# Attention with two gated MLPs: low parts of weights on VectorE, the PSUM banks of a pair apart, a re-timed engine order

## The chip, the cores and the metric

The kernel runs on one core of a Trainium2 chip. The metric is the device time of one execution in microseconds, as the median of several runs. A core has TensorE (PE in the profile, with PEld for its weight loads), VectorE (DVE), ScalarE (ACT), GpSimd (POOL) and SyncE (SP, which here issues nearly all DMAs). TensorE writes to PSUM, in banks of 512 fp32 columns on each partition, and the other engines read the results from there.

## What is computed

```python
def attention(q, k, v, cap):                 # 4 batches, 12 heads, 448 positions, 64 per head
    s = cap * tanh(q @ k.T / sqrt(64) / cap)
    e = exp(s - max(s));  return (e / (sum(e) + 1e-9)) @ v
x = attention(...)                           # 1792 tokens x 768
h = relu(x @ w_in);  x = (h * h) @ w_out     # 768 -> 2048 -> 768
g = sigmoid(x @ w_gate)                      # 768 -> 1536
out = (g * (x @ w_val)) @ w_out2             # 1536 -> 768
```

## The kernel before

**Precision.** A product of fp32 matrices is made of three fast matmuls: both operands are split into a high part (`hi`, rounded by a copy on ScalarE) and a low part (`lo = x - hi`), and lo·hi, hi·lo and hi·hi are added up in PSUM (L785, L787, L788). For a weight block, `place_w` has ScalarE write the high part `wh`, and `low` (L774) then has GpSimd write `wl`, the low part, by one subtraction over 128x384 or 128x768 elements. For activations VectorE makes the low part (`gx`, `gy`, `b`, `t`, by the helper at L240).

**Stages.** Attention runs over 24 pairs of heads. For a pair, TensorE makes the scores (`scores`, in three rotating PSUM tiles `so`, `si`, `se`), ScalarE takes tanh and exp (`pt`), TensorE multiplies by v (`pv`, L405, four steps), and then sums the rows of `pt` by matmuls with ones (`totals`, L420). The products and the sums of a pair lie in the two banks of one PSUM tile `pv`. VectorE copies the products out into `xe[:, 0]` once the four steps are done and the sums into `xe[:, 1]` after `totals` (both by L249); only after the second copy is the tile given back (`flow.put("pvb")`), and the next pair's first v step needs it. The normalisation then goes by small DMAs (`sg`, `rd`, `th`).

The two MLPs follow in four stages (two halves of the tokens for each MLP). Blocks are multiplied with seven products instead of eight (a Strassen scheme), so sums and differences of weights (`sums`, on VectorE) and of activations (`t`, `g`) are made first. The weights come as 64-bit words: they are loaded (`w`), turned into fp32 by five steps on VectorE (L627 to L635; in the MLP stages the first of them is on ScalarE), written to DRAM, and read back as `pair` when needed.

**What sets the order.** The order in which each engine's instructions stand is fixed when the program is built. The class `Flow` holds a small event model: a job yields an engine, a length and a rank, and waits for events or buffers; each engine takes the waiting job with the lowest rank and, among equals, the oldest. The lengths come from formulas (`act`, `dve`, `dvep`, `dve1`, `landing`), and the instruction is written to the engine at the moment that the model starts it. TensorE's own order is a list: in attention, the items S (a score tile), V (a v step) and Q (the sums) of `order`; behind it the MLP's `units`, in turn. `pick` starts an attention item when the model has its inputs, and otherwise the next unit when that one is ready. On the chip each engine then runs its list in that order and waits at the head of it. The formulas of before lengthen VectorE's work while GpSimd is busy (`shared`).

**Sigmoid.** ScalarE's first sigmoid is at the start of the third stage, the gate of the second MLP; its function table is loaded there.

Of the kernel before, what the change touches and what calls it, by code (L numbers as in the profile page):

```python
# [32 lines left out]
LATE = 1.0, 2.0, 0  # L33
# [27 lines left out]
class Flow:  # L61
# [4 lines left out]
    LAG = 0.06  # L66

    def __init__(self, have):
# [3 lines left out]
        self.queue = {e: [] for e in ("ACT", "DVE", "POOL", "SP")}  # L72
        self.free = {e: True for e in self.queue}
        self.end = dict.fromkeys(self.queue, 0.0)
# [37 lines left out]
    def serve(self, engine):  # L112
# [5 lines left out]
        length = length() if callable(length) else length  # L118

        def end():  # L120
            self.free[engine] = True
            self.at(self.now + self.LAG, lambda: self.step(job))
            self.serve(engine)

        self.end[engine] = self.now + length
        self.at(self.now + length, end)
# [23 lines left out]
    @staticmethod  # L150
    def act(n):
        return 0.23 + n * 0.00083

    def dve(self, n):
        return lambda: self.shared(0.15 + n * 0.00104, 2.0)

    def dve1(self, n):
        return lambda: self.shared(0.16 + n * 0.0005, 1.5)
# [7 lines left out]
    def dvep(n):  # L166
        return 0.15 + n * 0.00105


    def landing(self, size, store=False, rate=330e3):  # L170
        begin = max(self.now + (1.5 if store and size > 2e5 else 0.7 if store else 1.3), self.pipe)
        self.pipe = begin + size / rate
        return self.pipe + 0.9 - self.now
# [3 lines left out]
def attn_mlp_kernel(ctx: ExitStack, tc: tile.TileContext, qk, v, cap, w1, w2, wg, wv, wo, out):  # L177
# [33 lines left out]

    ones = T("att", "ones", [P, SR])
# [3 lines left out]
    for x in range(WARM):  # L216
        nc.tensor.matmul(out=bank2("pv", "pv")[:SR, 0, :S], lhsT=ones, rhs=warm, start=True, stop=True)
    head = T("att", "head", [P, 2, SR])
    for j in range(2):
# [4 lines left out]
        "sb": 3, "pvb": 1, "v": NV, "qkh": 2, "qk": 2, "pt0": PT, "pt1": PT, "xe": XE, "th": TH, "sg": 2,  # L224
# [20 lines left out]
    def post(out, bank, sb, op=ALU.add, rank=0):  # L245
        return on("DVE", flow.dvep(cols(out)), lambda: nc.vector.tensor_tensor(out=out, in0=sb, in1=bank, op=op), rank)  # L246

    def copy_ps(out, in_, rank=0):
        return on("DVE", flow.dvep(cols(out)), lambda: nc.vector.tensor_copy(out, in_), rank)  # L249
# [5 lines left out]
    def dma(out, in_, size, store=False, rate=330e3, issue=0.42, rank=1):  # L255
# [1037 lines left out]
```

## Time and profile before

| | us |
|---|---|
| median of 3 runs (1147.27 to 1152.98) | 1149.09 |
| the profiled execution: its time | 1153.2 |
| its span, from the first to the last instruction | 1151.4 |
| TensorE busy | 1105.2 |
| VectorE busy | 886.5 |
| ScalarE busy | 685.1 |
| GpSimd busy | 502.8 |

The span is 1.8 us shorter than the execution's own time. Attention ends at about 208 us of the span. A row of a timeline tells when an instruction (or a run of equal ones) started, how long it took, its engine, its line and tiles and, in brackets, how long the engine sat idle before it and what ended that. Instructions of one engine overlap a little: the next VectorE instruction starts some 0.08 us before the one before it is reported ended. Matmuls of 448 columns start 0.20 us apart at the full clock, though each is reported as 0.36 us long.

### The profile page before, as it was taken

What the parts mean: (1) busy time and instruction counts of PE and PEld (TensorE: products, weight loads), DVE (VectorE), ACT (ScalarE), POOL (GpSimd) and SP (SyncE); (2) the same over time, 40 slices, a digit from 0 to 9 for tenths busy, and PEclk for the clock granted to TensorE, in tenths of its full rate; (3) what the DMA queues carried; (4) which work ended last, traced back from release to release, by engine and by line L of the source; (5) the groups of instructions that cost most, each with busy time, mean ns of one, the idle gap of its engine ahead of it and who ended that gap; (6) DMA issues with size and microseconds to landing.
All of it is one profiled execution on the core that took longest, in us unless ns stands there. A gap on an engine that the chain in (4) does not pass through costs nothing.

```text
span 1151.4 us, 16365 instructions
## 1 busy us (share of the span) xinstructions
PE 1105.2 (96%) x5706; PEld 919.1 (80%) x5706; DVE 886.5 (77%) x1178; ACT 685.1 (60%) x1153; POOL 502.8 (44%) x364
## 2 busy tenths in 40 slices
PE   9999999998999999999999989799899899999997
PEld 4444444788988999999999879699798799999996
DVE  4586787987989479679889999769998646257467
ACT  6877898665554557675747556455445355555351
POOL 0000100444444435354636266567564656565543
PEclk9999999999999999999999999899999999999999
DMA  4677785597777275888896344374456843241322
GB/s 140 207 247 259 244 264 172 189 306 231 238 243 247 104 249 195 293 300 282 313 318 206 133 169 160 111 249 162 156 184 245 296 147 98 83 125 48 123 70 96
DMA packets 83986, 227.44 MB, mean 198 GB/s; under 512 B 11840, under 2 KB 29888, under 8 KB 83904
## 3 DMA queue, kind: packets, MB, share of 16 engines
q1 hardware_dynamic: 83904, 226.40, 58.3%
q8 instruction: 45, 0.74, 0.3%
q14 instruction: 37, 0.30, 0.1%
HBM read 160.24 MB, written 65.95 MB: 196 GB/s over the span
## 4 chain that ended last, share of the span: by engine, by line
PE 62%; DVE 19%; DMA 9%; issue 4%; SPq 2%; ACT 2%; POOL 1%; DVEq 0%; ACTq 0%; POOLq 0%
PE pb L785 18%; PE pb L787 18%; PE pb L788 18%; PE pv L405 4%; DMA w<-in_w_dram 2%; DVE raw L633 2%; DVE gx L240 2%; DMA s_w<-raw 2%; DVE raw L635 2%; PE pv L420 2%; DVE g L240 2%; DVE sums L240 2%; DMA pair<-s_w 1%; POOL wl L776 1%; DVE raw L631 1%
## 5 line engine op out<-in xcount | busy, mean ns | idle before, releaser
L776 POOL TENSOR_TENSOR wl<-pair,wh 128x384 fp32r<-128x384 f32 (+1 forms) x182 | 276.4, 1529 | 387.5 <-ACT wh L237 381.7
L776 POOL TENSOR_TENSOR wl<-sums,wh 128x384 fp32r<-128x384 f32 (+1 forms) x172 | 228.0, 1337 | 242.8 <-ACT wh L237 229.7
L785 PE MATMUL pb<-gx,wl 128*128 128x448 f32 x564 | 206.5, 366 | 13.8 <-POOL wl L776 7.5
L787 PE MATMUL pb<-gx,wh 128*128 128x448 f32 x564 | 207.5, 368 | 4.6 <-DVE gx L240 4.5
L788 PE MATMUL pb<-gx,wh 128*128 128x448 f32 x564 | 206.5, 366 | 0.0
L785 PE MATMUL pb<-t,wl 128*128 128x448 f32 x480 | 176.0, 367 | 6.2 <-ACT cp L237 3.5
L787 PE MATMUL pb<-t,wh 128*128 128x448 f32 x480 | 175.5, 366 | 0.0
L788 PE MATMUL pb<-t,wh 128*128 128x448 f32 x480 | 175.2, 365 | 0.0
L237 ACT ACTIVATE wh<-pair 128x384 fp32r<-128x384 f32 (+1 forms) x182 | 110.8, 625 | 62.8 <-PE pb L788 46.1
L237 ACT ACTIVATE wh<-sums 128x384 fp32r<-128x384 f32 (+1 forms) x172 | 90.9, 540 | 89.3 <-PE pb L788 56.0
L240 DVE TENSOR_TENSOR gx<-g,gx 128x448 fp32r<-128x448 f32 x124 | 122.8, 999 | 23.4 <-ACT gx L237 23.2
L785 PE MATMUL pb<-b,wl 128*128 128x448 f32 x360 | 132.0, 367 | 4.7 <-ACT pb L237 3.0
L787 PE MATMUL pb<-b,wh 128*128 128x448 f32 x360 | 131.9, 366 | 0.8 <-DVE b L240 0.8
L788 PE MATMUL pb<-b,wh 128*128 128x448 f32 x360 | 131.3, 365 | 0.0
L785 PEld LDWEIGHTS pb<-gx,wl 128*128 128x128 f32 x564 | 106.7, 189 | 24.9 <-POOL wl L776 11.4
L787 PEld LDWEIGHTS pb<-gx,wh 128*128 128x128 f32 x564 | 106.1, 188 | 16.3 <-DVE gx L240 7.6
L788 PEld LDWEIGHTS pb<-gx,wh 128*128 128x128 f32 x564 | 106.5, 189 | 8.0
L785 PEld LDWEIGHTS pb<-t,wl 128*128 128x128 f32 x480 | 90.2, 188 | 17.0 <-POOL wl L776 6.4
L788 PEld LDWEIGHTS pb<-t,wh 128*128 128x128 f32 x480 | 90.2, 188 | 7.4
L787 PEld LDWEIGHTS pb<-t,wh 128*128 128x128 f32 x480 | 90.0, 188 | 7.4
L405 PE MATMUL pv<-pt,v 128*64 128x448 f32 x384 | 82.8, 575 | 10.5 <-DVE xe L249 8.8
L246 DVE TENSOR_TENSOR r<-cp,pb 128x448 f32<-128x448 f32 x80 | 49.2, 615 | 55.4 <-ACT cp L237 37.4
(103 smaller groups left out, 1925.9 us busy)
## 6 DMA issues: line engine op xcount, KB each, us to landing
w<-in_w_dram SPq DMA_DIRECT2D x32, 768.0 KB
pair<-s_w SPq DMA_DIRECT2D x56, 384.0 KB
s_w<-raw SPq DMA_DIRECT2D x32, 384.0 KB
qk<-in_qk_dram SPq DMA_DIRECT2D x23, 480.0 KB
w<-in_wg_dram SPq DMA_DIRECT2D x12, 768.0 KB
w<-in_wv_dram SPq DMA_DIRECT2D x12, 768.0 KB
w<-in_wo_dram SPq DMA_DIRECT2D x12, 768.0 KB
pair<-s_wo SPq DMA_DIRECT2D x24, 384.0 KB
```

Of the source, the lines that this page charges most:

```text
L237: return on("ACT", flow.act(cols(out)) + extra, lambda: nc.scalar.activation(out=out, in_=in_, func=func, **kw), rank)
L240: return on("DVE", flow.dve(cols(out)), lambda: nc.vector.tensor_tensor(out=out, in0=a, in1=b, op=ALU.subtract), rank)
L246: return on("DVE", flow.dvep(cols(out)), lambda: nc.vector.tensor_tensor(out=out, in0=sb, in1=bank, op=op), rank)
L405: nc.tensor.matmul(out=o[j * D:(j + 1) * D, 0, :S], lhsT=st["v", n][:, c, j], rhs=pt, start=step == 0, stop=step == 3)
L420: nc.tensor.matmul(out=o[r:r + SR, 1, :S], lhsT=head[:, j] if step == 3 else ones, rhs=pt, start=step < 2, stop=step >= 2)
L631: yield on("DVE", flow.dve1(n), lambda: nc.vector.tensor_scalar(out=mu, in0=mu, scalar1=5, scalar2=2, op0=ALU.logical_shift_left, op1=ALU. ...
L633: yield on("DVE", flow.dve(n), lambda: nc.vector.scalar_tensor_tensor(out=mu, in0=lo, scalar=29, in1=mu, op0=ALU.logical_shift_right, op1= ...
L635: yield on("DVE", flow.dve(n), lambda: nc.vector.scalar_tensor_tensor(out=mu, in0=hi, scalar=0xC0000000, in1=mu, op0=ALU.bitwise_and, op1= ...
L776: yield on("POOL", 0.37 + n * 0.0022, lambda: nc.gpsimd.tensor_tensor(out=lo, in0=src, in1=f32(hi), op=ALU.subtract))
L785: nc.tensor.matmul(out=o, lhsT=wl, rhs=hi, start=first, stop=not stop, skip_group_check=not stop)
L787: nc.tensor.matmul(out=o, lhsT=wh, rhs=lo, start=False, stop=not stop, skip_group_check=not stop)
L788: nc.tensor.matmul(out=o, lhsT=wh, rhs=hi, start=False, stop=not stop or done_, skip_group_check=not stop)
```

## The change

Four things are changed together.

1. **Low parts of weights.** `low` calls `sub`, the VectorE subtraction, where it had a GpSimd instruction. GpSimd keeps only the memsets at the start.
2. **PSUM of a pair.** The two-bank tile `pv` becomes two tiles of one bank, `pvo` for the products and `pvs` for the sums, each with its own count in the model; `product` gives `pvo` back after the first copy, `result` gives `pvs` back after the second, and Q waits for `pvs`.
3. **Lengths in the model.** The formulas for VectorE no longer know of GpSimd; DMA landings go by kind (`LAND`); an engine is taken as free `OVER` before an instruction's result can be used. The order of VectorE, ScalarE and SyncE changes throughout, TensorE's in one place.
4. **Sigmoid table.** A sigmoid on one column, at unit 60 of the first MLP stage, is added on ScalarE (`first_sigmoid`). It writes `capa`, which nothing reads any more by then.

```diff
-    LAG = 0.06
+    LAG = 0.05
+    LAND = {"in": (270e3, 1.05), "load": (350e3, 1.15), "store": (350e3, 0.85), "th": (234e3, 1.3), "rd": (350e3, 1.4),
+        "sg": (350e3, 0.8)}
+    OVER = {"ACT": 0.1, "DVE": 0.08, "SP": 0.0}
...
-    def dve(self, n):
-        return lambda: self.shared(0.15 + n * 0.00104, 2.0)
...
-    def shared(self, length, slow):
-        if self.queue["POOL"]:
-            return length * slow
-        return min(length * slow, length + max(0.0, self.end["POOL"] - self.now) * (1 - 1 / slow))
+    def dve(n):
+        return 0.15 + n * 0.00104
...
+    def bank1(tag):
+        return open_pools["pv"][1].tile([P, 512], F32, tag=tag, name=tag, bufs=1)[:, :S]
...
     def pv(n, step):
         if step == 0:
-            st["o", n] = bank2("pv", "pv")
+            st["o", n] = bank1("pvo")
...
-        yield copy_ps(xe[:, 0], o[:, 0, :S])
+        yield copy_ps(xe[:, 0], o)
+        flow.put("pvo")
...
     def totals(n):
-        o = st["o", n]
+        o = bank1("pvs")
...
-        yield copy_ps(xe[:, 1], o[:, 1, :S])
-        flow.put("pvb")
+        yield copy_ps(xe[:, 1], o)
+        flow.put("pvs")
...
+    def first_sigmoid():
+        yield "until", ("unit", 60)
+        yield on("ACT", 1.5, lambda: nc.scalar.activation(out=capa, in_=qs, func=AF.Sigmoid), 0)
...
     def low(m, h, hi, lo, src, res, item):
         n = cols(src)
-        yield on("POOL", 0.37 + n * 0.0022, lambda: nc.gpsimd.tensor_tensor(out=lo, in0=src, in1=f32(hi), op=ALU.subtract))
+        yield sub(lo, src, f32(hi))
...
-            if kind == "Q":
+            if kind == "Q" and have("pvs"):
                 pe["a"] += 1
+                flow.have["pvs"] -= 1
```

VectorE's list at the tenth pair of attention, a pair during which a weight block is converted (`w` is the block as loaded, L627 to L635 the conversion, `xe<-pv` the copies out of PSUM). Before:

```order
L627 TENSOR_SCALAR raw<-w_861 128x768
L629 TENSOR_SCALAR raw<-raw 128x768
L631 TENSOR_SCALAR raw<-raw 128x768
L633 SCALAR_TENSOR_TENSOR raw<-w_861,raw 128x768
L249 COPY xe<-pv 128x448
L635 SCALAR_TENSOR_TENSOR raw<-w_861,raw 128x768
L249 COPY xe<-pv 128x448
```

And of the change:

```order
L627 TENSOR_SCALAR raw<-w_857 128x768
L629 TENSOR_SCALAR raw<-raw 128x768
L631 TENSOR_SCALAR raw<-raw 128x768
L244 COPY xe<-pvo 128x448
L633 SCALAR_TENSOR_TENSOR raw<-w_857,raw 128x768
L244 COPY xe<-pvs 128x448
L635 SCALAR_TENSOR_TENSOR raw<-w_857,raw 128x768
```

Each copy has moved ahead of one step of the conversion.

VectorE's list in the third stage, where the sums of the first block of the last weight matrix are made (`pair<-pair,sums` 128x768), with the conversions of two other blocks behind them. Before (GpSimd has the low parts in a list of its own, the block's first two being `wl<-sums,wh 128x768` and `wl<-pair,wh 128x768`):

```order
L240 TENSOR_TENSOR pair<-pair,sums 128x768
L240 TENSOR_TENSOR gx<-g,gx 128x448 x2
L629 TENSOR_SCALAR raw<-raw 128x768
L631 TENSOR_SCALAR raw<-raw 128x768 x2
L633 SCALAR_TENSOR_TENSOR raw<-w_7187,raw 128x768
L633 SCALAR_TENSOR_TENSOR raw<-w_7240,raw 128x768
L635 SCALAR_TENSOR_TENSOR raw<-w_7187,raw 128x768
L635 SCALAR_TENSOR_TENSOR raw<-w_7240,raw 128x768
```

And of the change:

```order
L235 TENSOR_TENSOR pair<-pair,sums 128x768
L235 TENSOR_TENSOR wl<-sums,wh 128x768
L629 TENSOR_SCALAR raw<-raw 128x768 x2
L631 TENSOR_SCALAR raw<-raw 128x768
L241 TENSOR_TENSOR r<-cp,pb_7244 128x448
L235 TENSOR_TENSOR wl<-pair,wh 128x768
L631 TENSOR_SCALAR raw<-raw 128x768
L235 TENSOR_TENSOR gx<-g,gx 128x448 x2
L633 SCALAR_TENSOR_TENSOR raw<-w_7201,raw 128x768
L633 SCALAR_TENSOR_TENSOR raw<-w_7236,raw 128x768
L235 TENSOR_TENSOR wl<-pair,wh 128x768
L235 TENSOR_TENSOR wl<-sums,wh 128x768
```

The low parts now stand in VectorE's list, two of them ahead of the conversions' long steps.

TensorE's list at the end of attention, from the last score tile on (`pb` are the MLP's banks). Before:

```order
L344 MATMUL se<-qkh 128x448
L405 MATMUL pv<-pt_2027,v 64x448 x4
L405 MATMUL pv<-pt_2045,v 64x448 x4
L420 MATMUL pv<-pt_2027,ones 32x448 x4
L420 MATMUL pv<-pt_2045,ones 32x448 x2
L420 MATMUL pv<-pt_2045,head 32x448 x2
L785 MATMUL pb_2147<-b_483,wl 128x448
```

And of the change, from the last pair's first v steps on:

```order
L400 MATMUL pvo<-pt_2082,v 64x448 x4
L785 MATMUL pb_2154<-b_464,wl 128x448
L787 MATMUL pb_2154<-b_464,wh 128x448
L788 MATMUL pb_2154<-b_464,wh 128x448
L785 MATMUL pb_2154<-b_1386,wl 128x448
```

Two units of the MLP, 18 matmuls, now stand between the first and the second half of the last pair's v steps. Elsewhere TensorE's order is as it was.

## Rows read from the trace of the kernel before

**Rows 1.** The page's busy times: engine, us (share of the span), instructions.
```profile
PE 1105.2 (96%) x5706; PEld 919.1 (80%) x5706; DVE 886.5 (77%) x1178; ACT 685.1 (60%) x1153; POOL 502.8 (44%) x364
```

**Rows 2.** TensorE waits: engine, line, releaser: us in total, times, longest.
```profile
PEld pb L785 <- POOL wl L776: 17.8, 9, 5.8
PEld pb L787 <- DVE gx L240: 7.6, 8, 2.9
PEld pv L405 <- DVE xe L249: 12.0, 9, 2.8
```

**Rows 3.** Timeline of TensorE in attention: start, us, instruction, [idle before <- releaser].
```profile
22.07 3.23 PE L405 MATMUL pv<-pt,v 128*64 128x448 f32 x16
29.70 3.23 PE L405 MATMUL pv<-pt,v 128*64 128x448 f32 x16
...
194.95 4.92 PE L405 MATMUL pv<-pt,v 128*64 128x448 f32 x16 [2.06 <-DVE xe L249]
203.71 3.23 PE L405 MATMUL pv<-pt,v 128*64 128x448 f32 x16 [1.38 <-ACT b L237]
```

**Rows 4.** Timeline of VectorE around the tenth pair.
```profile
90.58 0.56 DVE L627 TENSOR_SCALAR raw<-w 128x768 uint32<-128x768 uint32 x1 [3.87 <-DMA w<-in_w_dram]
...
91.77 0.56 DVE L631 TENSOR_SCALAR raw<-raw 128x768 uint32<-128x768 uint32 x1
...
93.24 0.62 DVE L249 COPY xe<-pv 128x448 f32<-128x448 f32 x1
...
94.64 0.62 DVE L249 COPY xe<-pv 128x448 f32<-128x448 f32 x1
```

**Rows 5.** Groups of instructions by form: count | busy us, mean ns | idle before.
```profile
L776 POOL TENSOR_TENSOR wl<-sums,wh 128x384 fp32r<-128x384 f32 x160 | 196.7, 1241 | 211.9 <-ACT wh L237 198.8 <-DMA w<-in_wv_dram 8.1 <-PE pb L785 4.4
...
L776 POOL TENSOR_TENSOR wl<-pair,wh 128x384 fp32r<-128x384 f32 x120 | 147.4, 1242 | 291.6 <-ACT wh L237 291.2
...
L776 POOL TENSOR_TENSOR wl<-pair,wh 128x768 fp32r<-128x768 f32 x62 | 129.1, 2086 | 95.9 <-ACT wh L237 90.5 <-PE pb L788 5.2
L240 DVE TENSOR_TENSOR gx<-g,gx 128x448 fp32r<-128x448 f32 x124 | 122.8, 999 | 23.4 <-ACT gx L237 23.2
...
L635 DVE SCALAR_TENSOR_TENSOR raw<-w,raw 128x768 uint32<-128x768 uint32 x68 | 83.2, 1225 | 0.8
...
L633 DVE SCALAR_TENSOR_TENSOR raw<-w,raw 128x768 uint32<-128x768 uint32 x68 | 82.8, 1221 | 1.3
...
L240 DVE TENSOR_TENSOR g<-g 128x448 f32<-128x448 f32 x60 | 60.5, 1008 | 0.8
...
L631 DVE TENSOR_SCALAR raw<-raw 128x768 uint32<-128x768 uint32 x68 | 54.7, 806 | 1.1
```

**Rows 6.** Timeline of VectorE in the third stage; GpSimd idle from 726.6 to 735.7.
```profile
720.92 2.27 DVE L240 TENSOR_TENSOR gx<-g,gx 128x448 fp32r<-128x448 f32 x1
...
726.99 0.94 DVE L635 SCALAR_TENSOR_TENSOR raw<-w,raw 128x768 uint32<-128x768 uint32 x1
...
730.12 0.62 DVE L240 TENSOR_TENSOR gx<-g,gx 128x448 fp32r<-128x448 f32 x1
...
731.19 0.95 DVE L243 TENSOR_TENSOR sums<-pair 128x768 f32<-128x768 f32 x1
```

**Rows 7.** Timelines of GpSimd, VectorE and TensorE right behind that.
```profile
735.72 8.17 POOL L776 TENSOR_TENSOR wl<-sums,wh 128x768 fp32r<-128x768 f32 x1 [9.13 <-ACT wh L237]
...
740.41 1.82 DVE L635 SCALAR_TENSOR_TENSOR raw<-w,raw 128x768 uint32<-128x768 uint32 x2
...
743.95 0.74 PE L785 MATMUL pb<-gx,wl 128*128 128x448 f32 x1 [5.40 <-POOL wl L776]
```

**Rows 8.** Stretches: us, busy time and (instructions) of each engine, granted clock, DMA.
```profile
500.00:900.00 400.00, 382.53 (x1856) 348.27 (x1855) 360.95 (x447) 227.15 (x427) 226.57 (x150) 0.99 0.61 214
...
738.00:750.00 12.00, 6.60 (x24) 5.67 (x23) 4.24 (x6) 3.70 (x7) 9.52 (x3) 0.72 0.00 0
```

**Rows 9.** Timeline of ScalarE at the first gate.
```profile
664.12 1.28 ACT L237 ACT_TABLE_LOAD   x1
```

More of the change, by code (lines that the diff above doesn't have):

```diff
@@ L71, in __init__ @@
         self.done, self.until = {}, []
-        self.queue = {e: [] for e in ("ACT", "DVE", "POOL", "SP")}
+        self.queue = {e: [] for e in ("ACT", "DVE", "SP")}
         self.free = {e: True for e in self.queue}
-        self.end = dict.fromkeys(self.queue, 0.0)
         self.pipe = 0.0
@@ L117, in serve @@
         write()
-        length = length() if callable(length) else length
         def end():
             self.free[engine] = True
-            self.at(self.now + self.LAG, lambda: self.step(job))
             self.serve(engine)
-        self.end[engine] = self.now + length
-        self.at(self.now + length, end)
+        self.at(self.now + length + self.LAG, lambda: self.step(job))
+        self.at(self.now + max(0.02, length - self.OVER[engine]), end)
     def put(self, resource):
@@ L151, in act, with dve1, landing @@
     def act(n):
-        return 0.23 + n * 0.00083
-    def dve(self, n):
-        return lambda: self.shared(0.15 + n * 0.00104, 2.0)
-    def dve1(self, n):
-        return lambda: self.shared(0.16 + n * 0.0005, 1.5)
-    def shared(self, length, slow):
-        if self.queue["POOL"]:
-            return length * slow
-        return min(length * slow, length + max(0.0, self.end["POOL"] - self.now) * (1 - 1 / slow))
-    @staticmethod
[L166 to L173, printed above, removed]
+        return 0.19 + n * 0.00085 + (0.06 if n >= 896 else 0.0)
+    @staticmethod
+    def dve(n):
+        return 0.15 + n * 0.00104
+    @staticmethod
+    def dve1(n):
+        return 0.15 + n * 0.00053
+    def landing(self, size, kind="load"):
+        rate, after = self.LAND[kind]
+        self.pipe = max(self.now + 0.5, self.pipe) + size / rate
+        return self.pipe + after + DLAG - self.now
 @with_exitstack
@@ L216, in attn_mlp_kernel @@
     for x in range(WARM):
-        nc.tensor.matmul(out=bank2("pv", "pv")[:SR, 0, :S], lhsT=ones, rhs=warm, start=True, stop=True)
+        nc.tensor.matmul(out=bank1("pvo")[:SR], lhsT=ones, rhs=warm, start=True, stop=True)
     head = T("att", "head", [P, 2, SR])
@@ L401, in pv @@
         if step == 0:
-            st["o", n] = bank2("pv", "pv")
+            st["o", n] = bank1("pvo")
         o = st["o", n]
         for j, c, pt in keys_of(n, step):
-            nc.tensor.matmul(out=o[j * D:(j + 1) * D, 0, :S], lhsT=st["v", n][:, c, j], rhs=pt, start=step == 0, stop=step == 3)
+            nc.tensor.matmul(out=o[j * D:(j + 1) * D], lhsT=st["v", n][:, c, j], rhs=pt, start=step == 0, stop=step == 3)
         return product(n, o) if step == 3 else None
@@ L419, in totals @@
                 r = (2 * (step % 2) + j) * SR
-                nc.tensor.matmul(out=o[r:r + SR, 1, :S], lhsT=head[:, j] if step == 3 else ones, rhs=pt,
+                nc.tensor.matmul(out=o[r:r + SR], lhsT=head[:, j] if step == 3 else ones, rhs=pt,
                     start=step < 2, stop=step >= 2)
@@ L942, in shares2 @@
         else:
-            yield on("DVE", flow.dvep(w), lambda: nc.vector.tensor_tensor(out=acc, in0=o, in1=acc, op=ALU.add), 0)
+            yield on("DVE", flow.dve(w), lambda: nc.vector.tensor_tensor(out=acc, in0=o, in1=acc, op=ALU.add), 0)
         flow.fire(("out", grp, num))
@@ L950, in shares2 @@
             acc = st["acc", stage, x][:, off:off + w]
-            yield on("DVE", flow.dvep(w), lambda: nc.vector.tensor_tensor(out=acc, in0=o, in1=acc, op=ALU.add), 0)
+            yield on("DVE", flow.dve(w), lambda: nc.vector.tensor_tensor(out=acc, in0=o, in1=acc, op=ALU.add), 0)
         if num in ("2453" if tail else "243"):
@@ L958, in finish @@
         t0 = START[STAGES[stage][1]] + off
[L959 removed]
+        yield from dma(out[:, x, t0:t0 + w], acc, P * w * 4, "store", issue=0.33)
         left["acc", stage, x] = left.get(("acc", stage, x), 2) - 1
@@ L975, in total @@
         acc = st["acc", stage, c][:, off:off + w]
-        yield on("DVE", flow.dvep(w), lambda: nc.vector.tensor_tensor(out=acc, in0=o, in1=acc, op=ALU.add), 0)
+        yield on("DVE", flow.dve(w), lambda: nc.vector.tensor_tensor(out=acc, in0=o, in1=acc, op=ALU.add), 0)
         give(o)
@@ L982, in total @@
             return
-        yield from dma(yn[c][:, off:off + w], acc, P * w * 4, True)
+        yield from dma(yn[c][:, off:off + w], acc, P * w * 4, "store")
         flow.fire(("stored", "y", off // w, c))
```

53 lines of the change are left out of this document (26 added, 27 removed).

## The prediction, made before the changed kernel ran

> **What bounds the kernel now.** I began with the page's busy times: TensorE is busy 1105 us of a span of 1151, 96%, and no other engine is over 77% [rows 1]. So no work taken off another engine shortens the run by itself; what can be won is TensorE's idle time, 1151.4 - 1105.2 = 46 us, and the time in which its clock is low. Next I read who ended TensorE's waits [rows 2]. Three names matter: the low parts of weights from GpSimd (17.8 us in 9 waits), the low parts of activations from VectorE (7.6 us in 8), and in attention VectorE's copy out of PSUM (12.0 us in 9). Then the timelines, one for each kind. In attention a pair takes 29.70 - 22.07 = 7.63 us when nothing waits [rows 3]; three times the v steps start about 2.1 us late for the copy, and the block of v steps then takes 4.92 us where 3.23 is usual [rows 3]: the granted clock is at its lower level (1.2 GHz) after such a stop. The rows of VectorE before the first of these stops show why the copy was late: it stood behind a conversion, and that had waited 3.87 us for its block to land [rows 4].
>
> The groups and timelines of the MLP show a second thing. VectorE's `gx` takes 0.62 us while GpSimd is idle and 2.27 beside a low part of GpSimd [rows 6], and its mean over the run is 1.00 [rows 5]. It works the other way too: a `wl` that began at 735.72 is reported as 8.17 us long where its kind takes 2.1 in the mean [rows 5, 7], and it ended 1.7 us after VectorE's run of conversions did (740.41 + 1.82 = 742.23, against 743.89). It made nothing while VectorE was busy without a break. TensorE waited 5.40 us for it and then ran in a stretch with a mean granted clock of 0.72 [rows 7, 8].
>
> **The change part by part.**
>
> *A. PSUM of a pair in two tiles.* Now a pair's first v step needs only the copy of the products, not that of the sums behind it. At the tenth pair the first copy ended at 93.24 + 0.62 = 93.86 and the second at 94.64 + 0.62 = 95.26 [rows 4], so 1.4 of the 2.06 us go by the tile alone; and in the new list the copy stands one conversion step of 0.9 us earlier, which takes the rest. A stop that short, 0.7 us or less, is nearer to the wait of 1.38 at 203.71, after which the v block took its usual 3.23 us, than to the 2.06 before the 4.92 [rows 3], so I count the slow block as gone too. All of it: 3 x (2.06 + 4.92 - 3.23) + 1.38 = 12.6 us, the last term being the last pair's, which now has 18 matmuls of 0.20 us, 3.7 us, to cover it. What is left is VectorE at the head of its list waiting for a DMA (3.87 us [rows 4]), which no part of the change removes. I take 11; bounds 5 (the copies still come late, the clock still falls) and 12.6.
>
> *B. The starved low part at 735.* On VectorE it is one of its own instructions, placed ahead of the conversions' long steps; a 768-wide operation of two inputs from SBUF takes 0.95 us [rows 6]. The stop of 5.40 goes, and with it the low clock: (1 - 0.72) x 12 = 3.4 us [rows 8]. I take 8.8, the whole. Bound below: 4, if the two conversions come first after all and it waits 1.82 us and more for them [rows 7].
>
> *C. The other waits for low parts,* 17.8 - 5.8 = 12.0 us in 8 waits [rows 2]. A low part took GpSimd 1.24 us (384 wide) [rows 5]. On VectorE I take 0.55 for it, an estimate between the 0.62 of 448 columns and the 0.95 of 768 [rows 6] by length. That is 0.7 us sooner once it is its turn, but it has to wait for its turn. Half: 6, bounds 0 and 12. One of these waits stands behind the load of the sigmoid table, 1.28 us of ScalarE [rows 9], which now comes in the first MLP stage; its cover there is ScalarE's idle share, 40% [rows 1], so I cost it at nothing, and at 1.3 us if a high part stands right behind it.
>
> *D. Waits for low parts of activations,* 7.6 us [rows 2]. With GpSimd silent they take 0.62 instead of 1.00 in the mean [rows 5, 6]. Half: 4, bounds 0 and 7.6.
>
> *E. What VectorE now has to carry.* 280 low parts at 0.55 and 62 at 0.95 [rows 5, 6] are 154 + 59 = 213 us (a dozen more wide ones add 11). Against that the stretching goes. From five groups alone [rows 4 to 6]: `gx` 124 x (0.999 - 0.62) = 47; `g` 60 x (1.008 - 0.62) = 23; L635 68 x (1.225 - 0.94) = 19; L633, of the same form, 68 x (1.221 - 0.94) = 19; L631 68 x (0.806 - 0.56) = 17: together 125 us. Smaller groups of the same kind add to it. So VectorE goes from 886 to 985 us at most (86% of the span), and to about 900 at the other end if the smaller groups make up the rest; I expect some 930. It stays below TensorE over the whole, though not by much in the third quarter (below). The price on TensorE: its banks are read out by VectorE too, and a read may now find a low part of 0.55 us ahead of it. I take -4 us; bounds 0 and -14.
>
> Sum: 11 + 8.8 + 6 + 4 - 4 = 26 us. Against the profiled execution's own 1153.2 that is 1127; the median of the runs is 4.1 lower, 1149.1, so the forecast is 1149 - 26 = **1123 us**. With every upper bound it would be 1149 - 41 = 1108, with every lower one 1149 + 5 = 1154.
>
> The Trainium skill (Perfetto Trace Analysis, Optimizing Scalar/DVE Operations) speaks against this direction: where VectorE is saturated, it says, some work may be given to ScalarE or even GpSimd, though it adds that these two share a read port, so that moving work between them might not help. By its first half the change adds 213 us to 886 and VectorE would be at 1099, 95%, beside TensorE's 96%; by its second half the sum of E holds. The rows of `gx` bear out the second half.
>
> **The rivals.**
>
> *No change (about 1149).* The stops only change their engine: C and D stay whole since VectorE is as full as before, the copies stay behind late DMAs (A at 5), B at 8.8, and E at its -14. That gives 5 + 8.8 - 14, nil. For it: the DMA wait in the rows of the tenth pair, and that VectorE is at 361 of 400 us from 500 to 900 [rows 8]. Against it: the tile alone takes 1.4 of each 2.06, whatever VectorE's load.
>
> *Slower: VectorE becomes the bound from 500 to 900.* There are 150 low parts there and 361 us of VectorE [rows 8]. They bring 150 x 0.55 = 83 us and take away 226.6 / 502.8 of the 125, 56 us [rows 1, 8]: 388 of 400, so 12 us of slack by these five groups. In an in-order list each low part may also stand at the head and wait for ScalarE's high part; GpSimd stood idle 211.9 / 160 = 1.3 us before each of one group [rows 5], which cost nothing there. If VectorE lost 0.3 us before each, 45 us, it would be 33 us over, TensorE would wait that long, and with A and B still won (20 us) the time is 1149 + 13 = 1162. The point from which this beats the baseline by 0.5% is 0.25 us for each: 38 - 12 - 20 = 6. For it: how full the stretch is. Against it: ranks put PSUM reads first, the smaller groups give more slack than I counted, and the list is written by the moments at which the high parts are expected.
>
> *Half (about 1140).* A and B go as forecast, nothing else: C and D come back whole, E at its price, and part of A stays: 7 + 8.8 - 6, 10 us. This is faster too, by 0.9%.
>
> **How the numbers follow.** Forecast, 1108 to 1138: 0.62. Better than 1108: 0.03, since hardly more than 41 us is to be had. Half, 1138 to 1143: 0.10. No change, 1143 to 1155: 0.12. Slower, over 1155: 0.13. About 0.5% (6 us) is what a measurement of this kernel can tell from none, so faster 0.75, same 0.12, slower 0.13. The range leaves out 0.03 below and some 0.17 above: the slower case and the upper third of no change. It is 1108 to 1150.
>
> **What would show each step.** A: no wait of TensorE's v steps for `xe` over 1 us and no v block of 4.9 us in attention; the first unit's matmuls behind attention some 11 us earlier. B: no stop over 3 us in the third stage and a granted clock of 1.00 from 700 to 750. C and D: the waits of L785 and L787 for the low parts, now both by VectorE, at 15 us together or less instead of 25. E: `gx` at 0.62 us in the mean, the conversion's steps at 0.94 and 0.56, VectorE's busy time between 900 and 985. I am wrong if VectorE is busy over 97% from 500 to 900 with TensorE's waits named after it, or if a low part at the head of VectorE's list waits for ScalarE while PSUM reads queue behind it.

## The result: 29 us faster, and the profile after

The changed kernel takes 1121.68 us as the median of four runs (1117.42 to 1122.41), against 1151.03 us of the kernel before (four runs, 1147.27 to 1154.45: the three of the table above and one more). The ratio is 0.9738, with a 95% interval of 0.9695 to 0.9781. The forecast was 1123, so the number held. Its reasons held only in part, and most of what follows is about that. One of the ten runs of `i3_late_w`, an experiment below, took 3347.93 us where the other nine took 1156 to 1161; it is left out of that kernel's ratio.

The profiled execution took 1117.42 us and is the fastest of the four; the profiled one of before was 2.2 us above the median of before. So the two traces are 35.8 us apart in span where the medians are 29.4 apart, and a few microseconds of what the traces show are scatter.

The page's busy times of the changed kernel (engine, us, share of the span, instructions) answer to [rows 1]:

```profile
PE 1097.2 (98%) x5706; PEld 919.6 (82%) x5706; DVE 899.1 (81%) x1532; ACT 688.3 (62%) x1154; POOL 1.1 (0%) x10
```

TensorE's idle time went from 1151.4 - 1105.2 = 46.2 us to 1115.6 - 1097.2 = 18.4, 27.8 us less, and its busy time fell by 8.0 us with the same 5706 matmuls, in part because less of them ran at the lower clock (the mean granted clock of the span is 0.996, before 0.992). VectorE carries 354 instructions more and is busy only 12.6 us longer.

Waits of TensorE's weight loads (PEld; line, releaser: us in total, times, longest), for comparison with [rows 2]:

```profile
PEld pb L785 <- ACT cp L232: 7.6, 10, 1.4
...
PEld pb L785 <- ACT pb L232: 4.1, 4, 2.5
...
PEld pb L787 <- DVE gx L235: 1.5, 1, 1.5
...
PEld pvo L400 <- DVE xe L244: 0.6, 2, 0.3
PEld pb L785 <- DVE wl L235: 0.6, 1, 0.6
```

The low parts of weights and of activations made TensorE's weight loads wait 25.4 us before; now 2.1. The copy out of PSUM in attention made them wait 12.0; now 0.6. In the MLP stages ScalarE is now at the head, with 7.6 and 4.1 us.

The matmuls' own waits (PE) for the same two causes are shorter, first before and then in the changed kernel:

```profile
PE pb L785 <- POOL wl L776: 10.1, 6, 5.4
...
PE pb L787 <- DVE gx L240: 4.5, 4, 2.5
```

```profile
PE pb L787 <- DVE gx L235: 1.3, 1, 1.3
...
PE pb L785 <- DVE wl L235: 0.2, 1, 0.2
```

TensorE itself stood still for the low parts for 14.6 us before and for 1.5 now.

VectorE's groups by form (count | busy us, mean ns | idle before them), for comparison with [rows 5]:

```profile
L235 DVE TENSOR_TENSOR wl<-sums,wh 128x384 fp32r<-128x384 f32 x160 | 86.3, 551 | 29.4 <-ACT wh L232 29.1
L235 DVE TENSOR_TENSOR gx<-g,gx 128x448 fp32r<-128x448 f32 x124 | 76.0, 619 | 14.7 <-ACT gx L232 13.9
L635 DVE SCALAR_TENSOR_TENSOR raw<-w,raw 128x768 uint32<-128x768 uint32 x68 | 64.7, 952 | 0.3
...
L235 DVE TENSOR_TENSOR wl<-pair,wh 128x768 fp32r<-128x768 f32 x62 | 59.1, 954 | 15.5 <-ACT wh L232 15.0
...
L631 DVE TENSOR_SCALAR raw<-raw 128x768 uint32<-128x768 uint32 x68 | 37.7, 555 | 1.1
```

A 384-wide low part takes 0.55 us where GpSimd needed 1.24, a 768-wide one 0.95 instead of 2.09. And `gx` fell from 999 to 619 ns, the conversion's steps from 1225 to 952 (L635) and from 806 to 555 (L631): no form is stretched any more.

The stretches (us, busy time and instructions of PE, PEld, DVE, ACT, POOL, granted clock, DMA share, GB/s) for comparison with [rows 8]:

```profile
500.00:900.00 400.00, 397.29 (x1954) 366.08 (x1953) 357.34 (x620) 229.57 (x432) 0.00 (x0) 1.00 0.65 229
700.00:750.00 50.00, 50.00 (x248) 46.05 (x247) 46.46 (x77) 31.02 (x56) 0.00 (x0) 1.00 0.63 219
```

From 500 to 900 TensorE is idle for 2.7 us instead of 17.5, the clock never falls, and VectorE does 620 instructions in less time (357) than it took for 447 before (361).

### The profile page after: what moved, and what is told of

It is laid out like the page before. It is cut to its first block, busy times and chain, and to the rows that moved or that the text cites. A ratio compares the mean times of both kernels' runs of the same rounds, so it can differ in the third digit from the quotient of the medians.

```text
span 1115.6 us, 16096 instructions
## 1 busy us (share of the span) xinstructions
PE 1097.2 (98%) x5706; PEld 919.6 (82%) x5706; DVE 899.1 (81%) x1532; ACT 688.3 (62%) x1154; POOL 1.1 (0%) x10
## 4 chain that ended last, share of the span: by engine, by line
PE 75%; DVE 11%; DMA 9%; ACT 3%; issue 2%; SPq 1%; DVEq 0%; POOL 0%; ACTq 0%; POOLq 0%
PE pb L785 21%; PE pb L787 21%; PE pb L788 21%; PE pvo L400 5%; DMA s_w<-raw 2%; PE pvs L416 2%; DVE wl L235 2%; PE se L339 2%; PE so L339 2%; PE si L339 2%; DVE raw L635 1%; ACT wh L232 1%; DVE acc L976 1%; DMA sg<-xe 1%; DVE raw L633 1%
## 5 line engine op out<-in xcount | busy, mean ns | idle before, releaser
L785 PE MATMUL pb<-gx,wl 128*128 128x448 f32 x564 | 205.1, 364 | 0.0
L785 PE MATMUL pb<-t,wl 128*128 128x448 f32 x480 | 176.2, 367 | 4.3 <-ACT cp L232 4.0
L235 DVE TENSOR_TENSOR wl<-pair,wh 128x384 fp32r<-128x384 f32 (+1 forms) x182 | 123.5, 689 | 26.4 <-ACT wh L232 25.8
L785 PE MATMUL pb<-b,wl 128*128 128x448 f32 x360 | 132.6, 368 | 3.0 <-ACT pb L232 2.8
L235 DVE TENSOR_TENSOR wl<-sums,wh 128x384 fp32r<-128x384 f32 (+1 forms) x172 | 97.7, 579 | 31.9 <-ACT wh L232 31.5
L785 PEld LDWEIGHTS pb<-gx,wl 128*128 128x128 f32 x564 | 106.2, 188 | 8.9 <-ACT pb L232 0.6
L785 PEld LDWEIGHTS pb<-t,wl 128*128 128x128 f32 x480 | 90.2, 188 | 15.0 <-ACT cp L232 7.6
L235 DVE TENSOR_TENSOR gx<-g,gx 128x448 fp32r<-128x448 f32 x124 | 76.0, 619 | 14.7 <-ACT gx L232 13.9
L232 ACT ACTIVATE gx<-g 128x448 fp32r<-128x448 f32 x124 | 70.2, 573 | 20.1 <-DVE g L835 10.0
L232 ACT ACTIVATE raw<-w 128x768 f32<-128x768 f32 x57 | 51.4, 902 | 48.0 <-DMA s_w<-raw 25.3
```

Source lines behind the costliest of these rows:

```text
L232: return on("ACT", flow.act(cols(out)) + extra, lambda: nc.scalar.activation(out=out, in_=in_, func=func, **kw), rank)
L235: return on("DVE", flow.dve(cols(out)), lambda: nc.vector.tensor_tensor(out=out, in0=a, in1=b, op=ALU.subtract), rank)
L785: nc.tensor.matmul(out=o, lhsT=wl, rhs=hi, start=first, stop=not stop, skip_group_check=not stop)
```

## Where the time came from

To place the gain in the run, I numbered the matmuls of the first product (L785, 1476 in every kernel here, in the same order, counted from 0) by their starts in each trace, and took the differences to the trace of before. Positive is earlier. `e1`, `k1` and `k2` are experiments of the next section: low parts on VectorE alone; the same with one number of the model changed; the whole change without that number.

| L785 no. | before starts at, us | changed | e1 | k1 | k2 |
|---|---|---|---|---|---|
| 120 | 287.4 | 12.6 | 5.4 | -1.1 | 9.1 |
| 600 | 584.3 | 9.4 | 6.2 | 2.8 | 12.6 |
| 720 | 658.9 | 11.0 | 0.3 | 4.5 | 6.3 |
| 840 | 747.5 | 24.8 | 15.2 | 17.5 | 20.4 |
| 1020 | 861.1 | 28.0 | 17.4 | 21.5 | 24.5 |
| 1080 | 902.2 | 32.5 | -1.5 | 26.0 | 0.8 |
| last | 1146.4 | 35.8 | 0.3 | 29.6 | 3.8 |

Two rows tell most. Between 720 and 840 lies the stop of [rows 7]: every kernel with low parts on VectorE gains 13 to 15 us there. Between 1020 and 1080 `e1` and `k2` lose 19 and 24 us, and the other two gain 4.5.

## The experiments

They were run in three groups, each beside its own runs of the kernel before (medians 1151.71, 1150.37 and 1151.05): the parts one at a time, the new lengths, and the last number of these with the test on GpSimd. Ratios are to that kernel, with 95% intervals.

### The parts one at a time

**Low parts on VectorE alone (`e1_low_dve`).**

```diff
-        yield on("POOL", 0.37 + n * 0.0022, lambda: nc.gpsimd.tensor_tensor(out=lo, in0=src, in1=f32(hi), op=ALU.subtract))
+        yield sub(lo, src, f32(hi))
```

> The kernel before with the low parts of weights on VectorE alone; PSUM tile, the formulas of the model and the sigmoid as before. Port theory (GpSimd and VectorE hold each other up, the tile pv holds up attention, the new lengths add little): attention's stops stay, the stops of the MLP for low parts and the long one near 740 go, so about 1132 us, 1127 to 1137, and gx takes 0.62 us. Order theory (the re-timed order is what won): within 5 us of before, 1146 or more. VectorE-bound theory: slower than before.

Measured: 1151.92 us, 1.0008 (0.9984 to 1.0032). Nothing, although its `gx` takes 618 ns and GpSimd is silent. One row of TensorE's weight-load waits, and two of TensorE's own timeline, where the 17.4 us that it is ahead at no. 1020 went:

```profile
PEld pb L785 <- DVE wl L240: 27.7, 6, 12.1
```

```profile
873.91 0.74 PE L785 MATMUL pb<-gx,wl 128*128 128x448 f32 x1 [11.68 <-DVE wl L240]
894.82 0.74 PE L785 MATMUL pb<-gy,wl 128*128 128x448 f32 x1 [8.11 <-DVE wl L240]
```

The low parts now come too late from VectorE. That is not because VectorE lacked the time: its timeline ahead of the first of these stops has it idle.

```profile
864.82 0.62 DVE L240 TENSOR_TENSOR gy<-g,gy 128x448 fp32r<-128x448 f32 x1 [0.64 <-ACT gy L237]
869.84 0.56 DVE L629 TENSOR_SCALAR raw<-raw 128x768 f32<-128x768 f32 x1 [4.40 <-ACT raw L237]
870.44 0.56 DVE L631 TENSOR_SCALAR raw<-raw 128x768 uint32<-128x768 uint32 x1
871.03 0.96 DVE L633 SCALAR_TENSOR_TENSOR raw<-w,raw 128x768 uint32<-128x768 uint32 x1
872.02 0.96 DVE L635 SCALAR_TENSOR_TENSOR raw<-w,raw 128x768 uint32<-128x768 uint32 x1
872.90 0.95 DVE L240 TENSOR_TENSOR wl<-pair,wh 128x768 fp32r<-128x768 f32 x1
```

The low part that TensorE waits for stands in the list behind the conversion of the last weight block, and that block had just been asked for: the conversion's first step, on ScalarE, waits for it to land.

```profile
868.92 0.89 ACT L237 ACTIVATE raw<-w 128x768 f32<-128x768 f32 x1 [4.13 <-DMA w<-in_wo_dram]
```

These are SyncE's issue of that load in `e1`, and in the changed kernel:

```profile
860.74 0.42 SPq L614 DMA_DIRECT2D w<-in_wo_dram  x1
```

```profile
780.81 0.33 SPq L614 DMA_DIRECT2D w<-in_wo_dram  x1
```

In `e1` the last block is loaded 80 us later than in the changed kernel (and 14 us later than before, 846.42). Something in the change brings the conversions forward; this was the question for the later experiments. (At a smaller stop of `e1`, 5.19 us long and ended at 653.96, VectorE works without a break and reaches the low parts late; there the order alone is at fault.)

**Two PSUM tiles alone (`e2_banks`).**

```diff
-            st["o", n] = bank2("pv", "pv")
+            st["o", n] = bank1("pvo")
...
-        yield copy_ps(xe[:, 0], o[:, 0, :S])
+        yield copy_ps(xe[:, 0], o)
+        flow.put("pvo")
...
-        flow.put("pvb")
+        flow.put("pvs")
```

> The kernel before with the pair's PSUM in two tiles alone. Port theory: only attention is shortened, the first MLP matmul behind it some 10 us earlier than at 208.5, and the time about 1141 us, 1137 to 1145; the long low part in the third stage may stay or not, as GpSimd meets VectorE differently. Order theory: the copies stay late in VectorE's list, so the stops in attention stay and the time is within 4 us of before.

Measured: 1148.71 us, 0.9990 (0.9964 to 1.0017), so between 4 us faster and 2 slower. The stops in attention shrink (waits for `xe` from 12.0 to 8.3 us), but two big ones stay, one of them with the slow block behind it:

```profile
92.44 3.23 PE L408 MATMUL pvo<-pt,v 128*64 128x448 f32 x16 [2.02 <-DVE xe L252]
126.67 4.75 PE L408 MATMUL pvo<-pt,v 128*64 128x448 f32 x16 [3.65 <-DVE xe L252]
```

The tile alone doesn't bring the copy forward when the copy stands behind a conversion whose block lands late: VectorE's waits for such blocks are 22.3 us in 9 here, against 12.6 in 5 before.

**Both (`e3_both`):** the edits of `e1` and `e2` together, with the old lengths in the model.

> The kernel before with both, low parts on VectorE and two PSUM tiles; the other formulas of the model and the sigmoid as before. Port theory: nearly the whole gain, 1120 to 1127 us. Order theory: at least 10 us short of it, 1132 or more, since the new lengths and the early table are missing.

Measured: 1148.53 us, 0.9964 (0.9937 to 0.9992). The late low parts of `e1` are back (27.9 us in 6 waits), at the same places. So parts 1 and 2 of the change make some 4 of its 29 us, 7 at most by the interval; the rest needs part 3 or 4.

**The changed kernel with low parts back on GpSimd (`e4_low_pool`).**

```diff
-        yield sub(lo, src, f32(hi))
+        yield on("POOL", 0.37 + n * 0.0022, lambda: nc.gpsimd.tensor_tensor(out=lo, in0=src, in1=f32(hi), op=ALU.subtract))
```

> The changed kernel with the low parts back on GpSimd, everything else as changed; the model knows GpSimd's own lengths but nothing of the two engines holding each other up. Port theory: attention's 10 us stay won, the rest is lost again and some more since the order does not know of it: 1138 to 1155 us, gx at about 1.0 us in the mean. Order theory: 1127 us or less.

Measured: 1184.99 us, 1.0285 (1.0239 to 1.0331), 63 us above the changed kernel. `gx` is at 880 ns again:

```profile
L235 DVE TENSOR_TENSOR gx<-g,gx 128x448 fp32r<-128x448 f32 x124 | 108.0, 880 | 49.5 <-ACT gx L232 49.3
```

The new lengths, which leave GpSimd out, are worse than the old ones as soon as GpSimd works. So part 3 without part 1 loses, and part 1 without part 3 gains nothing.

### Which of the new lengths

My first guess was the landings: the model of before expects a block earlier than it comes, and VectorE's list then waits for it. If so, the old landings in the changed kernel should lose, and a later landing in `e3` should win.

**Old landings in the changed kernel (`i1_old_land`), and 3 us more for a weight block in `e3` (`i3_late_w`).**

```diff
-        rate, after = self.LAND[kind]
-        self.pipe = max(self.now + 0.5, self.pipe) + size / rate
-        return self.pipe + after + DLAG - self.now
+        rate = {"th": 135e3, "form": 250e3}.get(kind, 330e3)
+        store = kind in ("store", "rd")
+        begin = max(self.now + (1.5 if store and size > 2e5 else 0.7 if store else 1.3), self.pipe)
+        self.pipe = begin + size / rate
+        return self.pipe + 0.9 + {"sg": 1.0, "th": 2.0}.get(kind, 0) - self.now
```

```diff
-            flow.spawn(convert(key, w64, flow.landing(P * n * 8) + LATE[2] * ("mlp" not in flow.done)))
+            flow.spawn(convert(key, w64, flow.landing(P * n * 8) + 3.0))
```

> The changed kernel with the old formula for the landing of DMAs (with its additions for the normalisation), everything else as changed. Landing theory (with low parts on VectorE the order only fits if the model knows when DMAs land; with the old formula a low part stands behind a conversion whose block lands late): 1138 us or more, with stops of over 4 us for low parts from 640 us on. Engine-length theory (the new lengths of ScalarE and VectorE did it): 1127 or less. Draw theory (each small shift of the model draws another order, and the changed kernel's is a lucky one): any time between.

> The kernel before with low parts on VectorE and two PSUM tiles (1148.5 us measured), and the model told that weight blocks land 3 us later than its old formula says; all else as there. Landing theory: the two stops of 12 and 8 us for low parts at 862 and 887 us go, and the time is 1120 to 1132. Engine-length theory: within 5 us of 1148. Draw theory: between, with stops of over 4 us at other places.

Measured: 1115.76 us, 0.9697 (0.9649 to 0.9745), for the first, and 1158.89 us, 1.0070 (1.0045 to 1.0096), for the second. The old landings lose nothing, and later ones make the waits for low parts longer (37.5 us in 6). My guess fell.

**Landings 0.3 us earlier in the changed kernel (`i2_dlag0`).**

```diff
-DLAG = 0.3
+DLAG = 0.0
```

> The changed kernel with DLAG at 0 for 0.3, so that the model has every DMA land 0.3 us sooner. Landing theory: the order hardly cares for 0.3 us where blocks land 5 to 9 us after their issue; 1118 to 1128 us. Draw theory: another draw, 8 us or more away from 1122.

Measured: 1112.15 us, 0.9672 (0.9625 to 0.9720). It is the fastest kernel here, and faster than the one before beyond doubt. Its interval overlaps a little with that of the changed kernel (0.9695 to 0.9781), so I don't claim more than a few microseconds between those two, and know no mechanism for them.

**One PSUM tile in the changed kernel (`i4_old_psum`):** part 2 undone, the rest kept.

```diff
-            st["o", n] = bank1("pvo")
+            st["o", n] = bank2("pv", "pv")
...
-        yield copy_ps(xe[:, 0], o)
-        flow.put("pvo")
+        yield copy_ps(xe[:, 0], o[:, 0, :S])
...
-        flow.put("pvs")
+        flow.put("pvb")
```

> The changed kernel with a pair's products and sums in one PSUM tile again, everything else as changed. Tile theory (term A of the prediction): attention's stops for the copies come back, the first MLP matmul behind attention some 8 us later, about 1131 us. If the new lengths had removed those stops: 1125 or less. Draw theory: the order behind attention changes too, and stops turn up there as well.

Measured: 1120.73 us, 0.9739 (0.9692 to 0.9786): the same as the changed kernel. Its trace does have the stops in attention again, such as

```profile
62.72 3.23 PE L400 MATMUL pv<-pt,v 128*64 128x448 f32 x16 [2.18 <-DVE xe L244]
```

and is 8.3 us later than the changed one at the 120th L785. But that profiled run was the slowest of its four, and the changed kernel's the fastest. What the tile is worth in the median, somewhere between 0 and some 7 us by these intervals, stays open.

### The 0.08 us between two VectorE instructions

One number of part 3 was left. The old model frees VectorE when an instruction is reported ended. The new one frees it 0.08 us earlier (`OVER`). In the changed kernel's timeline of VectorE it can be read off:

```profile
705.01 0.56 DVE L235 TENSOR_TENSOR wl<-sums,wh 128x384 fp32r<-128x384 f32 x1
705.49 0.62 DVE L835 TENSOR_TENSOR g<-r 128x448 f32<-128x448 f32 x1
706.02 0.95 DVE L238 TENSOR_TENSOR sums<-pair 128x768 f32<-128x768 f32 x1
706.89 0.62 DVE L235 TENSOR_TENSOR g<-g 128x448 f32<-128x448 f32 x1
```

The starts are 0.48, 0.53 and 0.87 us apart, where 0.56, 0.62 and 0.95 are reported. The old formula, 0.15 + 0.00104 n, gives 0.55 for 384 and 0.95 for 768: the reported lengths. The 0.08 us holds for instructions that don't need each other's result. The conversion's steps in the rows of `e1` above, each on the `raw` of the one before, start 0.60, 0.59 and 0.99 us apart where 0.56, 0.56 and 0.96 are reported. So over 1532 instructions at most 123 us of VectorE are believed taken by the old model and are not. My theory: a model that thinks VectorE full lets the work of low rank, which the conversions are, slip until they are urgent.

**`e1` with this number (`k1_low_dve_over`), the changed kernel without it (`k2_no_over`), the kernel before with it (`k3_over_only`).** The first and the third have the edit below; the second sets `"DVE": 0.0` in `OVER`.

```diff
         def end():
             self.free[engine] = True
-            self.at(self.now + self.LAG, lambda: self.step(job))
             self.serve(engine)
...
-        self.at(self.now + length, end)
+        self.at(self.now + length + self.LAG, lambda: self.step(job))
+        self.at(self.now + max(0.02, length - 0.08 * (engine == "DVE")), end)
```

> The kernel before with low parts on VectorE (1151.9 us measured) and one number more: the model lets VectorE start its next instruction 0.08 us before the last one ends, as the trace shows it. Overlap theory (without it the model holds VectorE for fuller than it is, so conversions, which have the last rank, are put off, and low parts wait for their weights): the last weight block is loaded near 790 us and not at 861, no stop of over 4 us for low parts, 1115 to 1128 us. If the other new lengths were needed too: 1140 or more. Draw theory: between, with long stops elsewhere.

> The changed kernel with VectorE's 0.08 us taken out of the model again, all else as changed. Overlap theory: the last weight block is loaded 50 us later or more, long stops for low parts from 640 us on, 1140 us or more. If ScalarE's lengths or the landings carry it: 1127 or less.

> The kernel before with the 0.08 us alone, low parts still on GpSimd. Both needed (the order fits only a VectorE that GpSimd doesn't hold up): 1140 us or more, gx at about 1.0 us. Order alone enough: 1130 or less.

| kernel | low parts on | 0.08 in the model | median us | ratio (95%) |
|---|---|---|---|---|
| before | GpSimd | no | 1151.05 | 1 |
| `k3_over_only` | GpSimd | yes | 1157.92 | 1.0059 (1.0033 to 1.0085) |
| `e1_low_dve` | VectorE | no | 1151.92 | 1.0008 (0.9984 to 1.0032) |
| `k1_low_dve_over` | VectorE | yes | 1122.35 | 0.9747 (0.9701 to 0.9793) |
| changed | VectorE | yes | 1121.68 | 0.9738 (0.9695 to 0.9781) |
| `k2_no_over` | VectorE | no | 1150.74 | 1.0009 (0.9982 to 1.0036) |

The two together bring the whole gain, and neither alone brings any of it. `k3` asks for the last weight block at 804.38 us, 42 us sooner than before, and is no faster for it. `k1` has no second PSUM tile, no new landings and no early sigmoid, and is where the changed kernel is. `k2` has all of these, and is where the kernel before is. From 700 to 900 us the stretches of `e1`, `k1` and `k2`, in this order, differ in TensorE's busy time by over 20 us:

```profile
700.00:900.00 200.00, 178.80 (x860) 163.34 (x859) 171.88 (x289) 99.10 (x185) 0.00 (x0) 0.96 0.59 201
```

```profile
700.00:900.00 200.00, 199.98 (x985) 184.28 (x984) 179.15 (x310) 106.74 (x198) 0.00 (x0) 1.00 0.64 223
```

```profile
700.00:900.00 200.00, 177.13 (x844) 162.12 (x843) 170.67 (x284) 97.79 (x180) 0.00 (x0) 0.94 0.57 201
```

VectorE is *less* busy in the two slow ones. The last weight block is asked for at 860.74 us in `e1` and at 851.11 in `k2`, against 789.34 in `k1` and 780.81 in the changed kernel. `k2` stops where `e1` does:

```profile
852.04 0.74 PE L785 MATMUL pb<-b,wl 128*128 128x448 f32 x1 [9.80 <-DVE wl L235]
870.81 0.74 PE L785 MATMUL pb<-gx,wl 128*128 128x448 f32 x1 [4.34 <-DVE wl L235]
892.27 0.74 PE L785 MATMUL pb<-gy,wl 128*128 128x448 f32 x1 [8.10 <-DVE wl L235]
```

Nor is it a lucky order (the draw theory of the expectations) that divides them. Of the nine kernels here with low parts on VectorE and nothing added, the five with the 0.08 (changed, `k1`, `i1`, `i2`, `i4`) take 1112 to 1122 us and ask for the last block at 775 to 789 us; the four without it (`e1`, `e3`, `i3`, `k2`) take 1149 to 1159 and ask at 851 to 870. Landings, tile and sigmoid differ within both groups; they, or the draw, may explain the 10 us inside a group. No other value than 0 and 0.08 was run.

The plan itself shows the same. When the program is built, the model has a time for its own end and for every unit; it is no measurement, but it tells what the list was written for:

| | plan's end, us | span on the chip, us |
|---|---|---|
| before | 1120.0 | 1151.4 |
| `e1` | 1155.0 | 1151.1 |
| `k1` | 1119.4 | 1121.8 |
| `k2` | 1129.3 | 1147.6 |
| changed | 1094.2 | 1115.6 |
| `e4` | 1093.9 | 1183.4 |

In the plan of `e1` two neighbouring units start 21.1 us apart (at 856.0) and two others 10.8 (at 886.9), where 2 is usual. The chip's stops at 862 and 887 were written into the list: the model could not fit the low parts in, and put TensorE's wait there. From 780 us to that first gap VectorE has no pause at all in the plan of `e1`; in the plan of `k1` it is busy for 86% of the same time, and on the chip `e1` itself has it busy for 68.62 of these 76 us, 90%. So the plan of `e1` does take VectorE for full where it isn't. `e4` shows the opposite error, a plan that doesn't know how GpSimd and VectorE hold each other up and is missed by 90 us.

### GpSimd beside VectorE

**The changed kernel with idle work on GpSimd (`k4_port`).** For each low part, GpSimd also multiplies a 128x384 tile of its own by itself. Nothing waits for that, and it is added work, nothing is left out.

```diff
         yield sub(lo, src, f32(hi))
+        nc.gpsimd.tensor_tensor(out=idle_t, in0=idle_t, in1=idle_t, op=ALU.mult)
```

> The changed kernel, and 354 multiplications of 128x384 on GpSimd over a tile of its own, that nothing waits for; the order of all other engines is as changed. Port theory: while they last (425 us at 1.2 us each, more if VectorE holds them up) VectorE's operations with SBUF inputs are stretched, gx above 0.8 us there and 0.62 behind them, and TensorE waits more: 1135 us or more. If VectorE has room for it: 1127 or less.

Measured: 1227.91 us, 1.0667 (1.0617 to 1.0716), 106 us above the changed kernel. GpSimd ran its 354 instructions one behind another from 2.1 to 450.6 us. The stretches of this kernel:

```profile
0.00:210.00 210.00, 179.93 (x1142) 80.58 (x1142) 187.18 (x222) 153.08 (x161) 196.71 (x173) 0.94 0.58 195
210.00:500.00 290.00, 229.71 (x1032) 192.69 (x1033) 264.68 (x289) 123.39 (x218) 225.59 (x193) 0.88 0.51 164
500.00:900.00 400.00, 397.95 (x1953) 365.66 (x1952) 353.58 (x611) 254.42 (x480) 0.00 (x0) 1.00 0.68 238
```

TensorE is idle for 30.1 us in the first stretch and 60.3 in the second, where the changed kernel has 5.6 and 5.9, and its clock is lower there (0.94 and 0.88, against 0.99); from 500 on, with GpSimd done, it is as busy as in the changed kernel. VectorE's `gx` from 0 to 460 us, and after that, by groups:

```profile
L237 DVE TENSOR_TENSOR gx<-g,gx 128x448 fp32r<-128x448 f32 x23 | 26.0, 1139 | 0.1
```

```profile
L237 DVE TENSOR_TENSOR gx<-g,gx 128x448 fp32r<-128x448 f32 x101 | 62.0, 621 | 14.1 <-ACT gx L234 13.6
```

The engine order is that of the changed kernel and no data pass between the two engines, so the price of GpSimd's company is shown by itself: `gx` at 1139 ns beside it and 621 without.

## Why the prediction was right, and where it was not

**What bounds the kernel:** right. TensorE's idle time and low clock were what could be won, 46.2 us of idle time, and 27.8 of it went.

**B, the starved low part at 735:** right, and the firmest term. All four kernels of the table above gain 13 to 15 us between the 720th and 840th L785, which holds B's 8.8 and a part of C, and the granted clock from 700 to 750 is 1.00 where before it was 0.93, with 0.72 from 738 to 750 [rows 8]. `e2`, with GpSimd still at work, gains nothing there.

**C and D, the other low parts:** taken at 6 and 4, as half of 12.0 and 7.6 us. Those are waits of weight loads. By its matmuls TensorE stood still for them, without B's 5.4 us, for 4.7 and 4.5, together 9.2, and 7.7 of that went. The 10 came out near because half of the weight loads' waits is nearly all of the matmuls' own. And it holds only with the new lengths; with the old ones C returns as 27.7 us (`e1`).

**E, VectorE's load and its price:** the load was bounded well and expected too high, the price has the wrong sign. 221.2 us of low parts came (123.5 + 97.7 by the page's two groups) and VectorE grew by 12.6: 208.6 us of stretching went, where five groups gave 125, so at 899.1 it is just below the lower end of the 900 to 985. The price of -4 for PSUM reads queued behind low parts is a gain instead. These waits of TensorE were in the trace of before, and nothing answers to them in that of after:

```profile
PE pb L785 <- DVE acc L943: 4.4, 3, 2.4
...
PE pb L785 <- DVE r L246: 1.6, 2, 0.9
```

TensorE's waits for VectorE's reads of PSUM fell by 6.0 us, and `e1`, `k1` and `k2` have none of these either. I had taken the reads as hurt by what is put ahead of them. That they had stood behind stretched instructions before would explain the gain; I have no run that shows it alone.

**The step that failed: part 3 has no term.** The working is A to E, and the new lengths come in only as "the new list". I had written down myself that VectorE's next instruction starts some 0.08 us early, and did not ask what a planner does that lacks it. Parts 1 and 3 are one change: `e1` and `k3` are worth nothing or less, `k1` 28.7 us. My terms B to E, read as what low parts on VectorE bring, are refuted by `e1`; read as what they bring in a list that is written for VectorE's true pace, they are borne out by `k1`. The forecast held since the kernel as handed over had both.

**A, the PSUM tiles:** mis-sized as a term of its own. It was put at 11. The reading of [rows 3] left a stop for the copy out, longer than the three that it counted and without a slow block behind it:

```profile
62.66 3.23 PE L405 MATMUL pv<-pt,v 128*64 128x448 f32 x16 [2.38 <-DVE xe L249]
```

From 59 to 66 us the granted clock is 1.00. So a stop of some 2 us doesn't always bring the slow block. In the changed kernel's profiled run the matmuls behind attention do stand 12.6 us earlier (the 120th L785), and no block of v steps waits over 1 us for the copy. But the tile alone is worth at most 4 us (`e2`), undoing it costs nothing that four runs can tell (`i4`), and `k1` without it is as fast as the changed kernel. A stop for another reason even brings back a slow block; the changed kernel's timeline in attention:

```profile
123.41 0.73 PE L339 MATMUL se<-qkh,qkl 64*128 64x448 f32 x2 [3.02 <-ACT pt L232]
...
124.82 4.23 PE L400 MATMUL pvo<-pt,v 128*64 128x448 f32 x16
```

I had reckoned at the tenth pair that 1.4 us of each stop go by the tile alone; the stops of 2.02 and 3.65 us in `e2` show that they need not. So the sum came out because two errors nearly cancel, which is luck: A is some 7 to 11 us too high by `e2` (4 to 11 by `i4`), and B to E, 14.8 together, some 14 too low, since `k1`, without the tile, gains 28.7. Of these 14, E is some 10 (-4 taken, 6.0 gained in the traces); the rest I can't place.

**The rivals.** *Slower, VectorE as the bound:* VectorE's low parts do wait at the head of its list, as that rival said:

```profile
DVE wl L235 <- ACT wh L232: 57.3, 74, 2.7
```

That is 57.3 / 354 = 0.16 us for each, below the deciding 0.25, and VectorE is at 357 of 400 us from 500 to 900, 89% and not 97. `e1` has the same wait (56.5 us in 75), so it is not what made `e1` lose. *No change* is what parts 1 and 2 give with the old lengths, by a mechanism that I had not named.

**Sigmoid table:** in the changed kernel it is loaded at 302.90 us, in the first MLP stage, and no stop of TensorE stands near. I didn't run it alone; `k1` without it is 0.7 us from the changed kernel, within the scatter.

## What to carry to other kernels

Where a planner writes the order, the lengths that it plans with are part of the kernel: here, moving work onto an engine that the plan believed full gained nothing, although the trace showed room on it. Before moving, compare the start-to-start time of neighbouring instructions with the lengths in the plan, and look for the transfers that the plan puts off. And time a change in its parts *and* in pairs: here two parts that are each worth nothing are worth 29 us together.

## What the runs showed of the hardware

**VectorE's pace.** Back to back, VectorE starts instructions about 0.08 us before the one before is reported ended, for lengths from 0.55 to 0.95 us alike, where the second doesn't need the first one's result; where it does, it starts 0.03 to 0.04 us behind that end (the conversion's steps in `e1`). I knew the first as a detail; that it decides 29 us of 1150 (29.6 from `e1` to `k1`, 29.1 from `k2` to the changed kernel) I had not expected.

**Which VectorE instructions GpSimd's company stretches.** In `k4` GpSimd's own instructions come 30.61 / 25 = 1.22 us apart in this piece, and VectorE's timeline beside them reads:

```profile
394.58 30.61 POOL L779 TENSOR_TENSOR idle_t<-idle_t 128x384 f32<-128x384 f32 x25
```

```profile
404.84 0.61 DVE L979 TENSOR_TENSOR acc<-pb,acc 128x448 f32<-128x448 f32 x1
...
410.04 0.61 DVE L979 TENSOR_TENSOR acc<-pb,acc 128x448 f32<-128x448 f32 x1
...
411.14 1.18 DVE L237 TENSOR_TENSOR wl<-pair,wh 128x384 fp32r<-128x384 f32 x1
412.24 1.58 DVE L637 SCALAR_TENSOR_TENSOR raw<-w,raw 128x768 uint32<-128x768 uint32 x1
```

The low part takes 1.18 us instead of 0.55 and the conversion's step 1.58 instead of 0.95, both 0.63 us longer, while `acc`, which takes one input from PSUM, keeps its 0.61. A step with a single input from SBUF is stretched too: L633 in `k4`, the L631 of the changed kernel, from 555 ns to 999 in the mean of the first 460 us.

```profile
L633 DVE TENSOR_SCALAR raw<-raw 128x768 uint32<-128x768 uint32 x32 | 32.0, 999 | 0.7
```

The Trainium skill (SBUF — State Buffer, Who interferes with whom) says why: VectorE and GpSimd share one pair of ports; an operation of VectorE with two inputs from SBUF contends with a GpSimd instruction that reads there, one with a single such input, outside the two-port modes, does not; and in those modes the later of the two is blocked and not merely slowed. The rows of the low part, of the conversion's step and of `acc` agree with the first two. The third no run here shows by itself: the stretched L633 and the low part of [rows 7], which ended only after VectorE's run of conversions, would fit it, but L633's mode stands in no trace, and most of that run has two inputs from SBUF. What this company costs is in `k4`: 106 us for 354 small instructions for which nobody waits.
